# One decode block on one core: wq and w3 each fetched by one DMA instead of two, x by three instead of one

## Chip, core and metric

The kernel runs on one core of a Trainium2 chip. The metric is the device time of one execution in microseconds, the median of the runs shown. Nothing else runs on the core.

## What is computed

One decode step of a transformer block for four sequences, D = 1024, in bf16. The reference, cut to what matters:

```python
# x (4,1,1024); k_cache, v_cache (4,4,8192,128); wq (1024,4096); wo (4096,1024)
# w1, w3 (1024,3584); w2 (3584,1024); Hq = 32, Hkv = 4, Dh = 128
q = layernorm(x) @ wq                        # 32 heads of 128
k, v = the last W = 2048 positions of the caches, each kv head used by 8 q heads
p = softmax(q . k * Dh**-0.5)
h = x + (p . v) @ wo
n = layernorm(h)
out = h + (silu(n @ w1) * (n @ w3)) @ w2
```

Weights and the part of the caches that is read come to 55.6 MB, and every byte of it is used once.

## The kernel before

All big operands go through one SBUF buffer, `ring` (L88), 160 KiB in each of the 128 partitions. `plan` (L110) lists the transfers in their order, each with its place in `ring`; `load_next(n)` (L129) issues the next n entries. Each entry is a DMA from SP's queue through `load_rows` (L90: some consecutive weight rows per partition, in one contiguous run) or two DMAs through `load_kv` (L96: two sequences, 16 KiB per partition each). A place is used again and again, so that an entry may overwrite what an earlier one brought. The framework (Tile) derives waits from the order of the statements in the program and from the bytes of `ring` that they touch: a DMA waits for earlier readers and earlier writers of its bytes, and a matmul waits for the last DMA that stands ahead of it in the program and writes the bytes it reads. DMA completions are counted on eight semaphores, used in rotation over all DMAs of the SP and ACT queues; a DMA whose turn it is waits on SP until the DMA eight before it has landed.

Places in KiB per partition, and the statement at which each entry is issued. The same list for the changed kernel is in the section on the change.

| entry | bytes per partition | issued |
|---|---|---|
| wq rows 0-3, wq rows 4-7 | 0-32, 32-64 | head (`load_next(5)`, L138) |
| k of sequences 0-1, 2-3 | 64-96, 96-128 | head |
| v of sequences 0-1 | 128-160 | head |
| v of sequences 2-3 | 0-32 | in the q loop, after row 3 (L222) |
| wo, 32 rows of 2 KiB | 32-96 | in the k loop, after the 8th unit (L274) |
| w1, 8 rows of 7 KiB | 96-152 | after p.v of sequence 1 (L333) |
| w3 rows 0-3 | 0-28 | after p.v of sequence 3 (L333) |
| w3 rows 4-7 | 28-56 | in the wo loop, after row 11 (L360) |
| w2 rows 0-16 | 56-90 | after the wo loop (L362) |
| w2 rows 17-23, 24-26, 27 | 90-104, 104-110, 110-112 | in the w1 loop, after row 3 (L410) |

Compute runs in this order, each stage on what the previous one left. The layer norm of x (L156 to L174; x is loaded on ACT's queue into `x_sb`, L137, and again as `x_q`, L148). q = xn @ wq, 64 matmuls (L215), in the order of the rows. Sixteen k units: transposes (L263), copies on VectorE and ScalarE (L267, L269), scores (L248). Softmax (L280 to L304). p.v, 64 matmuls for each sequence (L326). The wo product, 128 matmuls in the order of the rows, 4 per row (L353). A second layer norm (L366 to L391). `gate_up` (L398) with w1, 64 matmuls, 8 per row, into `g_ps`; the silu of the gate on ScalarE and VectorE (L415 to L419); `gate_up` with w3 into `u_ps`. Their product and its transpose (L422, L425). The w2 product, 112 matmuls (L433), then the result's cast and store (L443, L444).

Of the kernel before, what the change touches and what calls it, by code (L numbers as in the profile page):

```python
# [19 lines left out]
def kernel(  # L20
# [13 lines left out]
    nc = tc.nc  # L34

    B, _, D = A_x.shape
# [12 lines left out]
    x_flat = A_x.flatten_outer_dims()  # L49
# [31 lines left out]
    RQ = 4  # L81
    BS = 2
    wq_v = A_wq.rearrange("(p i) n -> p (i n)", i=KC)
    wo_v = A_wo.rearrange("(p i) n -> p (i n)", i=IO)
    w1_v = B_w1.rearrange("(p i) n -> p (i n)", i=KC)
    w3_v = B_w3.rearrange("(p i) n -> p (i n)", i=KC)
# [9 lines left out]
    def load_kv(at, src, b):  # L96
# [11 lines left out]
    N_Q, N_F = Hq * Dh, F  # L108
    KIB = 512
    plan = [  # L110
        ("wq", load_rows, (0, wq_v, N_Q, 0, 4)),
        ("wq", load_rows, (32 * KIB, wq_v, N_Q, 4, 4)),
        ("k", load_kv, (64 * KIB, A_k_cache, 0)),
        ("k", load_kv, (96 * KIB, A_k_cache, 2)),
        ("v", load_kv, (128 * KIB, A_v_cache, 0)),
        ("v", load_kv, (0, A_v_cache, 2)),
        ("wo", load_rows, (32 * KIB, wo_v, D, 0, 32)),
        ("w1", load_rows, (96 * KIB, w1_v, N_F, 0, 8)),
        ("w3", load_rows, (0, w3_v, N_F, 0, 4)),
        ("w3", load_rows, (28 * KIB, w3_v, N_F, 4, 4)),  # L120
        ("w2", load_rows, (56 * KIB, w2_v, D, 0, 17)),
        ("w2", load_rows, (90 * KIB, w2_v, D, 17, 7)),
        ("w2", load_rows, (104 * KIB, w2_v, D, 24, 3)),
# [5 lines left out]
    def load_next(n=1):  # L129
        for _ in range(n):  # L130
            if cursor[0] < len(plan):
                kind, f, args = plan[cursor[0]]
                loaded.setdefault(kind, []).extend(f(*args))
                cursor[0] += 1

    x_sb = act.tile([B, D], BF16)
    nc.scalar.dma_start(out=x_sb[:], in_=x_flat)  # L137
    load_next(5)  # L138

    ident = const.tile([P, P], BF16)  # L140
    make_identity(nc, ident[:])
# [5 lines left out]
    for j in range(JG):  # L147
        nc.scalar.dma_start(  # L148
            out=x_q[QD * j : QD * (j + 1) : RS, :], in_=x_flat[:, j * CG : (j + 1) * CG]
# [7 lines left out]
    for c in range(2):  # L157
# [8 lines left out]
        out=xn[:], in0=x_sb[:], scalar1=mv[:, 0:1], scalar2=rstd[:, 0:1],  # L166
# [4 lines left out]
    for kc in range(KC):  # L171
# [15 lines left out]
        out=perm[:].rearrange("p (h dq) -> p h dq", dq=JG),  # L187
        in_=ident[:].rearrange("p (dq h) -> p h dq", dq=JG),
# [12 lines left out]
    for j in range(2, JG):  # L201
        nc.vector.tensor_tensor(
            out=same[:, 0, :], in0=same[:, 0, :], in1=ident[:, j * QD : (j + 1) * QD], op=ALU.add
# [6 lines left out]
    for kc in range(KC):  # L210
        wq_t = loaded["wq"][kc]
        for hf in range(CQ // 512):
            for g in range(JG):
                c0 = g * CQ + hf * 512
                nc.tensor.matmul(  # L215
                    q_ps[QD * g : QD * g + B, hf * 512 : (hf + 1) * 512],
                    lhsT=xnT[:, kc, :],
                    rhs=wq_t[:, c0 : c0 + 512],
                    start=(kc == 0),
                    stop=(kc == KC - 1),  # L220
                )
        if kc == RQ - 1:  # L222
            load_next()
    q_sb = act.tile([P, CQ], BF16)
    nc.vector.tensor_single_scalar(out=q_sb[:, :512], in_=q_ps[:, :512], scalar=qscale, op=ALU.mult)  # L225
    nc.scalar.mul(out=q_sb[:, 512:], in_=q_ps[:, 512:], mul=qscale)
# [1 line left out]
    for r in range(REP):  # L228
        nc.tensor.transpose(out=qt_ps[:, r, :], in_=q_sb[:, r * Dh : (r + 1) * Dh], identity=ident[:])
    nc.vector.tensor_copy(  # L230
        out=qz[:, :, : Hkv * QD].rearrange("p b (g z) -> p b g z", g=Hkv)[:, :, :, :REP],
        in_=qt_ps[:].rearrange("p r (g x) -> p x g r", g=Hkv)[:, :B, :, :],
# [24 lines left out]
    for u, (b, n) in enumerate(units):  # L257
        k_v = loaded["k"][b]
        kT = ktpool.tile([P, NJ, P], BF16, tag="kT")
        for t in range(NJ // TB):  # L260
            kt_ps = psA.tile([P, TB, P], BF16, tag=f"kt{nt % 4}")
            for jj in range(TB):
                nc.tensor.transpose(  # L263
                    out=kt_ps[:, jj, :], in_=k_v[:, n * NJ + t * TB + jj, :], identity=ident[:]
# [21 lines left out]
        out=Pm[:], in_=scores_ps[:], func=ACT.Exp, bias=nmax[:], scale=1.0, accum_out=rsum[:]  # L286
# [6 lines left out]
    for c in range(NSB):  # L293
# [4 lines left out]
        for g in range(Hkv):  # L298
            if g % 2 == 0:
                nc.vector.tensor_scalar(  # L300
                    out=z[:, :, g, :], in0=pt_ps[:], scalar1=mask[:, g : g + 1], scalar2=None, op0=ALU.mult
# [10 lines left out]
        out=Dm[:], in0=ident[:].rearrange("p (g b r) -> p b g r", g=Hkv, b=B),  # L312
# [38 lines left out]
    for i in range(IO):  # L351
# [34 lines left out]
        out=hn[:], in0=h1[:], scalar1=tot[:, 0:1], scalar2=rstd2[:, 0:1],  # L386
# [5 lines left out]
        out=hnT[:].rearrange("p k x -> p (k x)"), in_=hn[:].rearrange("q (c k) -> q k c", k=KC)  # L392
# [5 lines left out]
    def gate_up(kind, out_ps):  # L398
# [27 lines left out]
        out=hgT[:].rearrange("p i x -> p (i x)"),  # L426
        in_=hg[:].rearrange("q s c -> q (s c)").rearrange("q (c i) -> q i c", i=IF),
# [47 lines left out]
```

## Time and profile before

| | us |
|---|---|
| median of 3 runs | 138.12 |
| lowest, highest | 138.05, 138.14 |
| the profiled execution, its own time | 138.12 |
| its span, first to last instruction | 136.3 |
| around the span | 1.8 |
| busy: PE, DVE, ACT, POOL | 67.9, 42.6, 31.0, 1.7 |

All durations below are from the one profiled execution, and times of day in it count from the start of its span. PE is TensorE, DVE VectorE, ACT ScalarE, SP the engine that issues the DMAs of `ring`. In lists of groups and in the timeline a row gives the engine, the line, the operation, its output and inputs, the shapes and how many; in the timeline the first two columns are the start and the length in us, and square brackets hold the idle time of the engine before it and what ended it. In the chain of waits the columns are start, length, and what the time went to. Matmuls overlap, so that the time of a stretch is read from its start and length and not from a mean of one times their number.

### The profile page before, as it was taken

To read this page: it belongs to the slowest core of one execution; us is meant where nothing else is said; L and a number is where in the kernel's file an instruction comes from. 1 tells how busy PE (TensorE), PEld (TensorE's weight loads), DVE (VectorE), ACT (ScalarE), POOL (GpSimd) and SP (SyncE) were. 2 spreads that over 40 slices of the span, in tenths; PEclk is the share of its full clock that TensorE was granted. 3 is DMA by queue.
4 is the path that set the end of the run, shared out by engine and by line. 5 is a ranking of instruction groups with operands and counts; after the bars stand their busy time and mean duration, and the time that the engine had idled before them with its cause. 6 is when DMAs were issued, how large, how long until landed. Compare 5 with 4: busy or idle time off the path is not lost.

```text
span 136.3 us, 2302 instructions
## 1 busy us (share of the span) xinstructions
PE 67.9 (50%) x1035; PEld 42.9 (31%) x1035; DVE 42.6 (31%) x73; ACT 31.0 (23%) x36; POOL 1.7 (1%) x8
## 2 busy tenths in 40 slices
PE   0101803698989889105259538830096440900960
PEld 0100201274656565001149427610043210300840
DVE  6440000244444444609940030160000695070000
ACT  0400000155555646092944000000003300000001
POOL 5000000000000000000000000000000000000000
PEclk9999999999999999965555865897557777555577
DMA  5999899999999999997988989989799999989960
GB/s 156 462 462 443 385 413 418 423 447 423 428 437 409 437 437 423 435 582 341 538 385 365 524 365 442 459 353 522 328 412 463 434 437 447 429 388 409 426 261 5
DMA packets 2662, 55.75 MB, mean 409 GB/s; under 512 B 312, under 2 KB 344, under 8 KB 604
## 3 DMA queue, kind: packets, MB, share of 16 engines
q1 hardware_dynamic: 2592, 55.58, 95.3%
q8 instruction: 8, 0.13, 0.3%
q10 hardware_dynamic: 60, 0.02, 0.1%
q14 instruction: 2, 0.02, 0.0%
HBM read 55.59 MB, written 0.01 MB: 408 GB/s over the span
## 4 chain that ended last, share of the span: by engine, by line
DMA 58%; PE 21%; ACT 13%; DVE 5%; issue 1%; SPq 0%; ACTq 0%
DMA ring<-in_B_w_dram 42%; DMA ring<-in_A_wq_dram 16%; PE kt_ps L263 9%; ACT kT L269 6%; PE scores_ps L248 5%; ACT z L304 3%; PE q_ps L215 2%; PE g_ps L403 2%; DVE rmax L280 2%; ACT Pm L285 2%; PE OT_ps L326 2%; DVE pT L294 1%; DVE z L300 1%; ACT L285 1%; DVE q_sb L225 1%
## 5 line engine op out<-in xcount | busy, mean ns | idle before, releaser
L269 ACT COPY kT<-kt_ps 128x1024 bf16<-128x1024 bf16 x16 | 15.8, 1014 | 12.0 <-PE kt_ps L263 12.0
L263 PE MATMUL kt_ps<-ident,ring 128*128 128x128 bf16 x256 | 16.4, 219 | 0.0
L263 PEld LDWEIGHTS <-ring 128*128 128x128 bf16 x256 | 14.3, 98 | 5.0 <-issue 4.9
L267 DVE COPY kT<-kt_ps 128x1024 bf16<-128x1024 bf16 x16 | 11.1, 691 | 15.2 <-PE kt_ps L263 15.2
L215 PE MATMUL q_ps<-ring,xnT 128*4 128x512 bf16 x64 | 6.7, 596 | 12.0 <-DMA ring<-in_A_wq_dram 12.0
L403 PEld LDWEIGHTS <-hnT 128*32 128x32 bf16 x128 | 5.3, 137 | 23.1 <-issue 20.5
L248 PE MATMUL scores_ps<-kT,qz 128*32 128x512 bf16 x64 | 9.9, 609 | 3.1 <-ACT kT L269 3.1
L326 PE MATMUL OT_ps<-z,ring 128*128 128x32 bf16 x256 | 7.4, 185 | 6.7 <-ACT z L304 5.0
L403 PE MATMUL u_ps<-ring,hnT 128*32 128x448 bf16 x64 | 6.3, 572 | 8.3 <-DMA ring<-in_B_w_dram 8.3
L403 PE MATMUL g_ps<-ring,hnT 128*32 128x448 bf16 x64 | 5.4, 525 | 9.0 <-DMA ring<-in_B_w_dram 9.0
L433 PE MATMUL y_ps<-ring,hgT 128*32 128x256 bf16 x112 | 5.7, 370 | 8.4 <-DMA ring<-in_B_w_dram 8.3
L326 PEld LDWEIGHTS <-ring 128*128 128x128 bf16 x256 | 7.3, 103 | 7.4 <-issue 7.4
L433 PEld LDWEIGHTS <-hgT 128*32 128x32 bf16 x112 | 4.4, 129 | 10.3 <-issue 6.1
L215 PEld LDWEIGHTS <-xnT 128*4 128x4 bf16 x64 | 2.1, 116 | 16.2 <-issue 15.9
L353 PE MATMUL y_ps<-ring,o 128*32 128x256 bf16 x128 | 5.8, 365 | 2.0 <-DMA ring<-in_A_wo_dram 2.0
L443 ACT CAST res<-y_ps 128x256 bf16<-128x256 f32 x1 | 0.4, 372 | 26.5 <-PE y_ps L433 26.5
L304 ACT ACTIVATE z<-pt_ps,mask 128x512 bf16<-128x512 f32 x8 | 5.3, 687 | 3.5 <-DVE z L300 3.5
L225 DVE TENSOR_SCALAR q_sb<-q_ps 128x512 bf16<-128x512 f32 x1 | 0.7, 690 | 17.2 <-PE q_ps L215 17.2
L353 PEld LDWEIGHTS <-o 128*32 128x32 bf16 x128 | 4.8, 130 | 3.8 <-issue 3.1
L300 DVE TENSOR_SCALAR z<-pt_ps,mask 128x512 bf16<-128x512 f32 x8 | 5.5, 740 | 1.2 <-ACT z L304 0.8
L296 PE MATMUL pt_ps<-pT,perm 128*128 128x512 bf16 x4 | 2.4, 607 | 6.8 <-DVE pT L294 6.8
L417 DVE RECIPROCAL eg<-eg 128x896 f32<-128x896 f32 x1 | 5.8, 5753 | 0.0
(73 smaller groups left out, 40.5 us busy)
## 6 DMA issues: line engine op xcount, KB each, us to landing
ring<-in_A_wq_dram SPq DMA_DIRECT2D x2, 4096.0 KB, 16.8
ring<-in_A_k_cache_dram SPq DMA_DIRECT2D x4, 2048.0 KB, 25.5
ring<-in_A_v_cache_dram SPq DMA_DIRECT2D x4, 2048.0 KB, 40.2
ring<-in_B_w_dram SPq DMA_DIRECT2D x1, 7168.0 KB
ring<-in_B_w_dram SPq DMA_DIRECT2D x2, 3584.0 KB, 28.6
ring<-in_B_w_dram SPq DMA_DIRECT2D x1, 4352.0 KB
ring<-in_B_w_dram SPq DMA_DIRECT2D x1, 1792.0 KB
ring<-in_B_w_dram SPq DMA_DIRECT2D x1, 768.0 KB
```

What stands on the lines that cost most here:

```text
L215: nc.tensor.matmul(q_ps[QD * g : QD * g + B, hf * 512 : (hf + 1) * 512], lhsT=xnT[:, kc, :], rhs=wq_t[:, c0 : c0 + 512], start=(kc == 0), ...
L248: nc.tensor.matmul(scores_ps[QD * g : QD * (g + 1), n * 512 : (n + 1) * 512], lhsT=qz[:, b, g * QD : (g + 1) * QD], rhs=kT_v[:, g, :, :], ...
L263: nc.tensor.transpose(out=kt_ps[:, jj, :], in_=k_v[:, n * NJ + t * TB + jj, :], identity=ident[:])
L267: nc.vector.tensor_copy(out=kT[:, t * TB : (t + 1) * TB, :], in_=kt_ps[:])
L269: nc.scalar.copy(out=kT[:, t * TB : (t + 1) * TB, :], in_=kt_ps[:])
L300: nc.vector.tensor_scalar(out=z[:, :, g, :], in0=pt_ps[:], scalar1=mask[:, g : g + 1], scalar2=None, op0=ALU.mult)
L304: nc.scalar.mul(out=z[:, :, g, :], in_=pt_ps[:], mul=mask[:, g : g + 1])
L326: nc.tensor.matmul(OT_ps[:, b, :], lhsT=loaded["v"][b][:, j, :], rhs=PTz[j // NJ][:, (j % NJ) * B + b, :, :], start=(j == 0), stop=(j == J ...
L353: nc.tensor.matmul(y_ps[QD * j : QD * (j + 1), :], lhsT=o4[:, i, :, :].rearrange("p b s -> p (b s)"), rhs=loaded["wo"][i][:, j * CG : (j + ...
L403: nc.tensor.matmul(out_ps[QD * j : QD * (j + 1), hf, :HF], lhsT=hnT[:, k, :], rhs=loaded[kind][k][:, c0 : c0 + HF], start=(k == 0), stop=( ...
L417: nc.vector.reciprocal(out=eg[:], in_=eg[:])
L433: nc.tensor.matmul(y2_ps[QD * j : QD * (j + 1), :], lhsT=hgT[:, i, :], rhs=loaded["w2"][i][:, j * CG : (j + 1) * CG], start=False, stop=(i ...
```

## The change

The two entries of wq become one of 64 KiB per partition, and the two of w3 one of 56 KiB. `x_sb` is filled by three DMAs of 512, 256 and 256 columns. The head issues four entries instead of five, and the call inside the q loop moves behind that loop. The calls at L274, L333, L360, L362 and L410 are as they were.

```diff
-        ("wq", load_rows, (0, wq_v, N_Q, 0, 4)),
-        ("wq", load_rows, (32 * KIB, wq_v, N_Q, 4, 4)),
+        ("wq", load_rows, (0, wq_v, N_Q, 0, 8)),
...
-        ("w3", load_rows, (0, w3_v, N_F, 0, 4)),
-        ("w3", load_rows, (28 * KIB, w3_v, N_F, 4, 4)),
+        ("w3", load_rows, (0, w3_v, N_F, 0, 8)),
...
-    nc.scalar.dma_start(out=x_sb[:], in_=x_flat)
-    load_next(5)
+    for c0, c1 in ((0, 512), (512, 768), (768, D)):
+        nc.scalar.dma_start(out=x_sb[:, c0:c1], in_=x_flat[:, c0:c1])
+    load_next(4)
...
-        if kc == RQ - 1:
-            load_next()
+    load_next()
     q_sb = act.tile([P, CQ], BF16)
```

With 12 entries instead of 14 and the calls that stayed, the entries are issued at these statements:

| entry | bytes per partition | issued, changed kernel |
|---|---|---|
| wq | 0-64 | head (`load_next(4)`) |
| k of sequences 0-1, 2-3, v of 0-1 | as before | head |
| v of sequences 2-3 | 0-32 | after the q loop |
| wo | 32-96 | in the k loop, after the 8th unit |
| w1 | 96-152 | after p.v of sequence 1 |
| w3, 8 rows | 0-56 | after p.v of sequence 3 |
| w2 rows 0-16 | 56-90 | in the wo loop, after row 11 |
| w2 rows 17-23 | 90-104 | after the wo loop |
| w2 rows 24-26, 27 | 104-110, 110-112 | in the w1 loop, after row 3 (the third call finds the list empty) |

## The prediction

> **What bounds the kernel now.** I read the page's slices first, then its chain, then the chain in order of time.
>
> ```profile
> PE   0101803698989889105259538830096440900960
> ...
> PEclk9999999999999999965555865897557777555577
> DMA  5999899999999999997988989989799999989960
> ```
>
> ```profile
> DMA 58%; PE 21%; ACT 13%; DVE 5%; issue 1%; SPq 0%; ACTq 0%
> ```
>
> ```profile
> 1.16 21.35 DMA ring<-in_A_wq_dram
> ...
> 73.22 25.79 DMA ring<-in_B_w_dram
> ...
> 101.59 31.37 DMA ring<-in_B_w_dram
> ...
> 133.35 0.37 ACT res L443
> ```
>
> The DMA row has no hole from the second slice to the last but two, PE's row has many: the kernel lasts as long as 55.6 MB take (408 GB/s over the span), plus a start and a tail. Compute hides as long as each DMA is issued before the stream runs dry. The timeline shows how far each stage is behind its data:
>
> ```profile
> 13.05 3.58 PE L215 MATMUL q_ps<-ring,xnT 128*4 128x512 bf16 x32 [6.05 <-DMA ring<-in_A_wq_dram]
> 22.55 3.15 PE L215 MATMUL q_ps<-ring,xnT 128*4 128x512 bf16 x32 [5.92 <-DMA ring<-in_A_wq_dram]
> 82.25 5.76 PE L353 MATMUL y_ps<-ring,o 128*32 128x256 bf16 x128 [2.04 <-DMA ring<-in_A_wo_dram]
> 91.64 0.63 DVE L391 STREAM_TRANSPOSE hnT<-hn 128x256 bf16<-128x256 bf16 x1
> 115.98 3.17 PE L403 MATMUL u_ps<-ring,hnT 128*32 128x448 bf16 x32 [5.34 <-DMA ring<-in_B_w_dram]
> 126.30 3.82 PE L433 MATMUL y_ps<-ring,hgT 128*32 128x256 bf16 x68 [7.14 <-DMA ring<-in_B_w_dram]
> ```
>
> Every weight stage starts when its DMA lands (brackets). Two arrivals matter below: all of w3 is in by 115.98, w2 rows 0-16 by 126.30. SP's waits show what holds the issues:
>
> ```profile
> SPq L101 <- DMA ring<-in_A_wq_dram: 16.2, 2, 9.9
> SPq L93 <- PE OT_ps L326: 25.3, 2, 20.1
> ```
>
> The first is the rotation of eight completion semaphores (k of sequence 2 waited 9.9 us for wq's first half, though it shares no byte with it). The second is real: w1 and w3 wait for p.v.
>
> **What the Trainium skill says.** "DMA: Bandwidth & Descriptors", Anatomy of one DMA: semaphore waits are made by the issuing sequencer, the DMA engines do not wait. The trace agrees: SP sat 20.1 us on p.v while transfers went on. The same section prices a DMA at about 2.0 us plus its bytes at 436 GB/s. That was fitted on GpSimd's path; here x_sb's 8 KB, issued from ACT at 0.73, released bn_stats at 2.52: 1.79 us, which I use. The same page, Rules for kernel authors, advises at least 1 MiB per DMA for bandwidth. Halves of 4 and 3.5 MB are past that; the trace has 432 GB/s in 22.5 to 25.8 under k's 16 KiB runs and 428 in 82.2 to 88.1 under w1's 56 KiB runs, so longer runs promise nothing.
>
> **The change, part by part.**
>
> *x in three pieces.* Two more issues on ACT at 0.57 us delay the last piece and x_q by 1.2 us. xnT is ready at 7.2, so 8.4; wq now lands at 22.5: hidden by 14 us. Cost 0; without that cover 1.2.
>
> *wq as one DMA.* One DMA has one landing, 22.51, where the second half landed. The 32 matmuls that ran from 13.05 move behind it: q ends at 22.55 + 3.58 + 3.18 = 29.3 instead of 25.74, 3.6 us late, and so do k, softmax and p.v, which are PE and ACT bound. What they hold back is issues: v of 2-3 at about 26 (two rows read) or later, wo 39.7 + 3.6 = 43.3 with v in the stream to 61, w1 73.2 + 3.6 = 76.8 with wo in the stream to 82, w3 79.2 + 3.6 = 82.8 with w1 until 99. Each still meets a stream that is not dry; smallest cover 5 us at w1, less about 1 us from issue to first byte. Cost 0 on the stream.
>
> *The rotation.* With two more x DMAs ahead, the DMA eight places before k of sequence 1 is wq: SP holds it, and k and v behind it, to 22.5. The stream then has only k of sequence 0, 2.1 MB or 4.8 us; the next issue takes 0.6 us and starts about 1 us later. Cost 0. If instead k of sequence 0 falls on wq's semaphore, the stream is dry for about 1.8 us and everything moves by that.
>
> *w3 as one DMA, and the shifted calls.* Here is the cost. The merged entry goes out at L333, ahead of the wo loop in the program, and writes 0-56 KiB; wo's rows 0-11 lie at 32-56. The call after row 11 now issues w2 rows 0-16 into 56-90, wo's rows 12-28; the one after the loop w2 rows 17-23 into 90-104, which takes in w1's row 0 and the start of row 1. The later matmuls therefore read the new bytes (the wo product mostly w3's and w2's numbers, the first two w1 rows partly w2's), and each waits for the DMA that wrote them. That waits follow byte ranges shows in the kernel before: the first 32 q matmuls ran at 13.05 with half of wq outstanding.
>
> 1. w3 behind w1 in the stream: landing 115.98 as before. The wo loop, which began at 82.25, begins there. Queued behind it on PE: everything to the end. Its first 12 rows are 48 matmuls, 48/128 of 5.76 = 2.2 us, to 118.1.
> 2. w2 rows 0-16 need no wo matmul, so SP issues them right behind w3 (about 83): landing 126.30 as before. Rows 12-31, 80/128 of 5.76 = 3.6 us: wo ends at 129.90.
> 3. w2 rows 17-23 must wait for wo's rows 29-31, at 129.90; the stream is dry by then. 1.79 + 1.835 MB at 432 GB/s (4.25) = 6.04: landing 135.95. The second layer norm beside it takes 88.01 to 92.27 = 4.26 us, to 134.2, hidden by 1.8.
> 4. The gate's 64 matmuls, 99.06 to 104.50 = 5.44: 141.4. The last two w2 entries wait for w1's rows 1 and 2 and land before 141; the w2 product is much later.
> 5. The silu, 104.50 to 114.45 = 9.95 (table load, exp, add, a reciprocal of 5.75, product): 151.35. The w3 product, 6.3 us, runs beside it. Before, both hid under the stream.
> 6. L422 and L425, 119.20 to 122.03 = 2.83: 154.2.
> 7. The w2 product without waits, 3.82 + 1.11 + 0.92 = 5.85: 160.1.
> 8. From the last matmul to the span's end, 136.3 − 133.33 = 2.97: 163.05.
>
> The profiled execution takes 1.82 us around its span (138.12 − 136.3) and equals the median, so the sum is **164.9 us**, 26.8 over before.
>
> **Bounds.** Small ones: step 3's fixed part between 1.0 (first issue 0.73, first packets about 1.7) and 2.5 us (the store at 133.75 to the span's end); arrivals ±0.5. PE's pace follows the clock: 56 ns a matmul at clock 0.50 (68 in 3.82), 40 at 0.82 (28 in 1.11); over 80 wo, 64 gate and 112 w2 matmuls −2.5 to +2.0. If w2 rows 0-16 too waited for the wo loop, they would land at 121.7 + 1.8 + 10.3 = 133.8 and rows 17-23 at 138.1: +2.1. The rotation's other place: +1.8. Low 161.0, high 169.0.
>
> **Rivals.**
>
> *The orders do not bind (A).* Should a wo matmul keep its wait for wo's own DMA, or the issues really keep their old order, PE runs as before 3.6 us late. The wo loop begins at 85.9, hnT is at 96 before w1 lands at 99, and the w3 product as one block ends 115.98 + 6.3 = 122.3, its transpose at 125.1, 1.2 us before w2 lands at 126.30: the last landing stays at 132.97 and the time is 138.1, not slower. The point from which it decides: the wo loop must not need anything behind w1 in the stream, that is, start before about 98 (98 + 5.76 + 4.26 + 5.44 + 9.95 + 2.83 = 126.2, when w2 is in). For it: transfers would be the same bytes at the same rate. Against it: the waits seen, byte by byte and by program order. Chance 0.05.
>
> *Only w3's wait binds (B).* If wo waits for w3 but w2's overwriting costs nothing, wo ends at 115.98 + 5.76 = 121.7, w1's product starts at 126.0, ends at 131.4, silu 141.4, then 2.83, 5.85, 2.97: span 153.1, time 154.9. For it: w2 is at place 56 and more, behind w3. Against it: the same rule that binds w3 binds it. Chance 0.05.
>
> *A dry stream at the head (C)*, with all of the forecast: 164.9 + 1.8 = 166.7. It lies in the range. Against it: x's first DMA is issued first, and k of sequence 0 then falls on its semaphore. Chance 0.1.
>
> The forecast itself has 0.8.
>
> **How the numbers follow.** 161 to 169 holds the forecast and C with their bounds; A and B, 0.1, and a miss in size are left out. A measurement of this kernel can tell about 0.2%, 0.3 us; A would be within it mostly, with a little on either side: faster 0.01, same 0.04, slower 0.95.
>
> **What would show it.** Right: L353's first row waits for the DMA of a B weight and starts near 116, a second group near 126; SP waits long on the wo loop; the DMA slices are empty from about 126 to 131 and after 136; the chain ends PE, ACT, DVE (L417) and not in a DMA; L403 starts near 136. At the head, one L215 group of 64 at 22.5. Wrong: L353 starting by 86 (A), L403 by 127 (B), or a hole in the DMA row at 22 to 25 (C).

## Result and profile after

| | before | after |
|---|---|---|
| median, us | 138.13 (138.05 to 138.30, 6 runs) | 165.97 (164.81 to 166.59, 6 runs) |
| the profiled execution, us | 138.12 | 166.07 |
| its span, us | 136.3 | 164.3 |
| HBM read | 55.59 MB | 55.59 MB |

The ratio is 1.2002, 95% interval 1.1955 to 1.2048: the change costs 27.8 us (165.97 − 138.13). Where runs of one kernel lie more than 1.5% apart, its ratio is that of the shorter ones, which below concerns `e4_w3_early_only` alone.

The slices of the page of the changed kernel; each is 4.1 us:

```profile
PE   0000149989898803159300000000602839900192
...
PEclk9999999999999995555955555555595675995559
DMA  7997979999999999999799999998991091510000
```

DMA, which had no hole before, is full up to about 125 us, then comes in pieces, and is idle for the last 16 us. PE is empty from the 21st to the 28th slice, between p.v and wo. The same bytes at the same rate are nearly all in at the same time as before; what follows them is now compute.

The second half of the kernel in the timeline of TensorE:

```profile
116.28 2.75 PE L351 MATMUL y_ps<-ring,o 128*32 128x256 bf16 x48 [33.32 <-DMA ring<-in_B_w_dram]
126.44 4.07 PE L351 MATMUL y_ps<-ring,o 128*32 128x256 bf16 x80 [7.40 <-DMA ring<-in_B_w_dram]
...
134.82 3.92 PE L401 MATMUL u_ps<-ring,hnT 128*32 128x448 bf16 x37 [2.27 <-DVE hnT L389]
138.15 4.40 PE L401 MATMUL g_ps<-ring,hnT 128*32 128x448 bf16 x64
142.20 1.49 PE L401 MATMUL u_ps<-ring,hnT 128*32 128x448 bf16 x27
155.50 5.75 PE L431 MATMUL y_ps<-ring,hgT 128*32 128x256 bf16 x112 [11.81 <-DVE hgT L423]
```

The wo product (L351) began at 82.25 before, released by wo's own DMA. Now PE sits 33.32 us until a DMA of a B weight, w3, lands; then 48 matmuls, which are wo's rows 0-11, and again 7.40 us until w2 rows 0-16 land; then the other 80. By then these DMAs have written over the bytes that the rows 0-28 stood in, so that the product multiplies w3's and w2's numbers: the changed kernel no longer computes the block, and what is timed here is the wait that comes with this. Behind them one stage follows the other without cover, down to the w2 product (L431), which waits 11.81 us for VectorE and for no DMA. Among SP's waits, the issue of w2 rows 17-23 behind the wo loop stands out (us in all, times, longest); before, two waits on the wo product came to 5.5 us:

```profile
SPq L93 <- PE y_ps L351: 31.2, 1, 31.2
```

It ends at 130.55, 4.5 us after the stream ran dry (by the trace's packet records the last packet of w2 rows 0-16 ends at 126.1).

### The profile page after: what moved, and what is told of

Read it like the earlier page. It is cut to its first block, busy times and chain, and to the rows that moved or that the text cites. A ratio compares the mean times of both kernels' runs of the same rounds, so it can differ in the third digit from the quotient of the medians.

```text
span 164.3 us, 2303 instructions
## 1 busy us (share of the span) xinstructions
PE 66.0 (40%) x1035; PEld 41.7 (25%) x1035; DVE 42.5 (26%) x73; ACT 31.1 (19%) x36; POOL 1.7 (1%) x8
## 3 DMA queue, kind: packets, MB, share of 16 engines
HBM read 55.59 MB, written 0.01 MB: 338 GB/s over the span
## 4 chain that ended last, share of the span: by engine, by line
DMA 65%; PE 21%; DVE 8%; ACT 4%; issue 1%; SPq 0%; DVEq 0%; ACTq 0%
DMA ring<-in_B_w_dram 27%; DMA ring<-in_A_wo_dram 25%; DMA ring<-in_A_wq_dram 13%; PE kt_ps L261 4%; PE q_ps L214 4%; PE y_ps L431 4%; DVE eg L415 4%; PE y_ps L351 2%; PE u_ps L401 2%; PE g_ps L401 2%; ACT kT L267 2%; PE scores_ps L246 2%; DVE hgT L423 1%; ACT L413 1%; DVE hg L420 1%
## 5 line engine op out<-in xcount | busy, mean ns | idle before, releaser
L351 PE MATMUL y_ps<-ring,o 128*32 128x256 bf16 x128 | 6.8, 402 | 40.7 <-DMA ring<-in_B_w_dram 40.7
L261 PE MATMUL kt_ps<-ident,ring 128*128 128x128 bf16 x256 | 17.1, 220 | 0.0
L351 PEld LDWEIGHTS <-o 128*32 128x32 bf16 x128 | 5.3, 141 | 43.0 <-issue 42.1
L246 PE MATMUL scores_ps<-kT,qz 128*32 128x512 bf16 x64 | 10.5, 609 | 2.6 <-ACT kT L267 2.6
L431 PE MATMUL y_ps<-ring,hgT 128*32 128x256 bf16 x112 | 5.8, 401 | 11.8 <-DVE hgT L423 11.8
L214 PE MATMUL q_ps<-ring,xnT 128*4 128x512 bf16 x64 | 6.0, 559 | 4.7 <-DMA ring<-in_A_wq_dram 4.7
L431 PEld LDWEIGHTS <-hgT 128*32 128x32 bf16 x112 | 4.3, 143 | 13.5 <-DVE hgT L423 12.2
L171 PE MATMUL tp_ps<-ident,xn 4*128 4x4 bf16 x8 | 0.7, 199 | 17.3 <-DVE xn L164 17.3
L401 PE MATMUL u_ps<-ring,hnT 128*32 128x448 bf16 x64 | 5.4, 483 | 2.3 <-DVE hnT L389 2.3
L401 PEld LDWEIGHTS <-hnT 128*32 128x32 bf16 x128 | 3.9, 121 | 6.9 <-issue 3.0
L171 PEld LDWEIGHTS <-xn 4*128 4x128 bf16 x8 | 0.6, 163 | 17.3 <-DVE xn L164 17.3
```

Source lines behind the costliest of these rows:

```text
L214: nc.tensor.matmul(q_ps[QD * g : QD * g + B, hf * 512 : (hf + 1) * 512], lhsT=xnT[:, kc, :], rhs=wq_t[:, c0 : c0 + 512], start=(kc == 0), ...
L246: nc.tensor.matmul(scores_ps[QD * g : QD * (g + 1), n * 512 : (n + 1) * 512], lhsT=qz[:, b, g * QD : (g + 1) * QD], rhs=kT_v[:, g, :, :], ...
L261: nc.tensor.transpose(out=kt_ps[:, jj, :], in_=k_v[:, n * NJ + t * TB + jj, :], identity=ident[:])
L351: nc.tensor.matmul(y_ps[QD * j : QD * (j + 1), :], lhsT=o4[:, i, :, :].rearrange("p b s -> p (b s)"), rhs=loaded["wo"][i][:, j * CG : (j + ...
L401: nc.tensor.matmul(out_ps[QD * j : QD * (j + 1), hf, :HF], lhsT=hnT[:, k, :], rhs=loaded[kind][k][:, c0 : c0 + HF], start=(k == 0), stop=( ...
L431: nc.tensor.matmul(y2_ps[QD * j : QD * (j + 1), :], lhsT=hgT[:, i, :], rhs=loaded["w2"][i][:, j * CG : (j + 1) * CG], start=False, stop=(i ...
```

## Experiments

Seven kernels. A number of a line is that of the kernel's own text; wo is L351 or L352, the gate and w3 products L399 to L404. The theory is the one of the prediction: the calls that now issue an entry earlier make wo's and w1's products wait for transfers that overwrite their rows. The main rival is that the large DMAs, the late q or the late x cost part of it.

### The calls put back: e1_calls_back

```diff
-        if b % BS == BS - 1:
+        if b == BS - 1:
             load_next()
```

against the changed kernel; wq and w3 stay whole, x stays in three pieces.

> The changed kernel with wq and w3 whole and x in three pieces, but w3 issued in the wo loop after row 11 and w2 rows 17-23 in order behind it: the call at L331 of the changed kernel is made for sequence 1 only. No statement reads overwritten bytes. Theory (the shifted calls cost all of it): wo starts when PE is ready, near 86, the stream has no hole, the last landing stays near 133 and the time is 138.1 to 138.6; w3 as one block leaves some 1 us to w2's landing. Rival (the large DMAs, the late q or the late x cost part of it): q is 3 us later than before, so 141 to 142, or more.

Measured 138.19 us (14 runs, before 138.19 on the same chip), ratio 0.9999, interval 0.9990 to 1.0007. Its timeline of TensorE:

```profile
22.56 5.85 PE L214 MATMUL q_ps<-ring,xnT 128*4 128x512 bf16 x64 [4.59 <-DMA ring<-in_A_wq_dram]
...
83.62 6.06 PE L351 MATMUL y_ps<-ring,o 128*32 128x256 bf16 x128 [0.82 <-DVE o L340]
...
99.05 4.74 PE L401 MATMUL g_ps<-ring,hnT 128*32 128x448 bf16 x64 [7.33 <-DMA ring<-in_B_w_dram]
115.94 4.82 PE L401 MATMUL u_ps<-ring,hnT 128*32 128x448 bf16 x64 [12.16 <-DMA ring<-in_B_w_dram]
126.21 3.62 PE L431 MATMUL y_ps<-ring,hgT 128*32 128x256 bf16 x68 [5.45 <-DMA ring<-in_B_w_dram]
```

All of q waits for the one landing of wq, and q ends at 28.4 instead of 25.7. By wo the delay is 1.4 us (83.62 against 82.25), and at the gate it is gone: 99.05 against 99.06. w3's product, all behind one landing, ends at 120.8, and w2 still arrives at 126.21. The DMAs are those of the change and only the place of a call differs, so the whole loss is in the shifted calls; DMAs of 64 and 56 KiB runs neither gain nor cost more than 0.1% here.

### w3 alone: e2_w3_alone

The kernel before with the two w3 entries merged as in the change, nothing else edited.

> The kernel before with w3 alone merged and nothing else edited, so that all later calls issue one entry earlier, as in the change (the wo product and the first two rows of w1 read overwritten bytes, as there). Theory: the whole loss is here, wo's two groups start at 116 and 126.4, time 165 to 166.5. Rival (wq and x carry part of it): 161 to 163.

Measured 165.65 us, ratio 1.1971 (1.1923 to 1.2019), where the whole change has 1.2002 (1.1955 to 1.2048). wo's groups start at 115.87 and 126.08:

```profile
115.87 2.75 PE L352 MATMUL y_ps<-ring,o 128*32 128x256 bf16 x48 [33.27 <-issue]
126.08 4.46 PE L352 MATMUL y_ps<-ring,o 128*32 128x256 bf16 x80 [7.46 <-DMA ring<-in_B_w_dram]
```

The profile names no releaser for the first wait here; it ends within 0.4 us of where w3's landing ended it in the changed kernel (116.28). The one merged entry, with the calls that it shifts, carries the loss.

### wq and x alone: e3_wq_x_alone

The changed kernel with the two w3 entries of before.

> The changed kernel with w3 in two entries again, so that every later call issues what it did before; wq whole, x in three pieces. Theory: q, k, softmax and p.v run 3 us late, and nothing of it reaches the end: 138.0 to 138.4. Rival (late q pushes w1's issue to where the stream runs dry): 139 to 142, with a hole in the DMA row near 82.

Measured 138.32 us, ratio 1.0007 (0.9998 to 1.0016): no difference. wo starts at 83.72, the gate at 99.23, behind its DMA, and the page's DMA row has no hole near 82, which the rival needed.

### w3 early, w2 late: e4_w3_early_only

```diff
-        if i == 11:
-            load_next()
     load_next()
```

against the changed kernel.

> The changed kernel without the call in the wo loop: w3 still goes out ahead of the wo loop over wo's rows 0-11 (those rows of the product read w3's numbers), but w2 rows 0-16 only after the loop, and the rest of w2 in the w1 loop. Theory: wo starts at 116.2, all 128 matmuls 6.8 us to 123.0; second norm to 127.3, gate to 132.8, silu to 142.7, product and transpose to 145.6; w2 rows 0-16, issued at about 122.4, land by 134.5 to 138 and the rest by 146; end of span 154.5, time 156.3. Rival (w3's overwriting alone makes the loss): 164 to 166.

Measured 154.69 us (median of four runs, 152.86 to 155.81); the ratio, 1.1102 (1.1055 to 1.1148), comes from two of them and is 153.4 us beside 138.19. The timeline is that of the run of 155.19 us:

```profile
116.18 6.27 PE L351 MATMUL y_ps<-ring,o 128*32 128x256 bf16 x128 [33.33 <-DMA ring<-in_B_w_dram]
...
126.77 5.66 PE L399 MATMUL g_ps<-ring,hnT 128*32 128x448 bf16 x64 [2.27 <-DVE hnT L387]
```

wo waits once, for w3, and runs through. The steps behind it come as the sum had them, but the sum, 156.3, is above all four runs. In the profiled one, 1.1 below it, the 128 matmuls took 6.27 us instead of 6.8 and the w2 product 4.92 instead of the prediction's 5.85. So with w3's early issue alone the loss is 15.2 us (153.4 − 138.2), or 16.5 by the median of all four; rival B of the prediction, in which w3's wait alone binds, had 154.9 for the whole time.

### w2 early, w3 in its place: e7_w2_early_only

```diff
-        if b % BS == BS - 1:
+        if b == BS - 1:
             load_next()
...
         if i == 11:
-            load_next()
+            load_next(2)
```

against the changed kernel.

> The changed kernel with w3 issued in the wo loop after row 11, together with w2 rows 0-16, which still come ahead of wo's rows 12-28; w2 rows 17-23 behind the loop as in the change. So w3 overwrites nothing that is read later, w2 rows still do (wo's rows 12-28 and w1's first two read w2's numbers). Theory: wo's rows 0-11 run near 86, rows 12-31 again wait for w2's landing at 126.4, everything behind that as in the changed kernel: 165 to 166.5, no gain from w3's repair alone. Rival (the two waits add): w3's repair gives back the first of them, 138 + about 10 to 17 = 148 to 156.

Measured 165.05 us, ratio 1.1957 (1.1898 to 1.2016), which cannot be told from the change's. Its TensorE:

```profile
83.50 2.75 PE L351 MATMUL y_ps<-ring,o 128*32 128x256 bf16 x48 [0.81 <-DVE o L340]
126.08 4.46 PE L351 MATMUL y_ps<-ring,o 128*32 128x256 bf16 x80 [39.83 <-DMA ring<-in_B_w_dram]
```

The first twelve rows run at 83.50, 33 us earlier than in the changed kernel, and it buys nothing: the 80 that follow wait 39.83 us for w2. The two waits lie one behind the other on the same chain, and the later one contains the earlier. Taking away w3's gains nothing while w2's is there; taking away those of w2 (e4, where rows 17-23 go out late as well) gains 12.6 us (165.97 − 153.4; 11.3 by the median of all four runs); taking away all (e1) gains all.

### No issue behind the wo loop: e6_no_third

```diff
         if i == 11:
             load_next()
-    load_next()
```

against the changed kernel.

> The changed kernel without the call behind the wo loop: w2 rows 17-23 go out in the w1 loop after row 3, with the rest of w2, and no w1 row is overwritten before it is read (wo's rows 0-28 still read w3's and w2's numbers). Theory: wo ends at 130.5 as in the changed kernel, w1's product starts right behind the second norm at 134.8 with no w3 matmuls ahead of it, silu starts at 140.2 instead of 142.6, the w2 product near 153; 163.0 to 164.5, that is 1.5 to 3 below the changed kernel. Rival (the wait on w2 rows 17-23 is what delays the gate by all of the 6 us from 130.5 to landing): more than 3 below. Rival (hidden beside the norm anyway): 165.5 to 166.5.

Measured 163.05 us, ratio 1.1798 (1.1726 to 1.1870). The difference of the ratios, 0.0204, is 2.8 us; the intervals do not meet, so the rival at nothing falls, but they leave 1.2 to 4.4 us, so the time alone does not exclude the rival of more than 3. The timeline does. Its TensorE:

```profile
135.06 6.08 PE L400 MATMUL g_ps<-ring,hnT 128*32 128x448 bf16 x64 [2.27 <-DVE hnT L388]
140.98 3.19 PE L400 MATMUL u_ps<-ring,hnT 128*32 128x448 bf16 x64
```

The gate follows the norm directly, and w3's matmuls all come behind it. It starts 3.1 us before that of the changed kernel (135.06 against 138.15), not 6: the third overwriting adds only what the norm beside it does not cover. In these two executions the gain shrinks to 1.4 us by the gate's end, since the gate took 6.08 us here, at a granted clock of 0.51 (135.0 to 141.1), and 4.40 there, at 0.77 (138.2 to 142.5). The expectation, with a gate of 5.4, had the w2 product near 153; it starts at 154.09.

### x alone: e5_x_alone

The kernel before with x in three pieces, nothing else.

> The kernel before with x in three pieces alone; wq in two DMAs of 32 KiB runs. In the changed kernel x's third piece landed near 14.7 us and its packets came one per 2.43 us on their engines, the length of one 64 KiB packet of wq. Theory (each small packet waits for one packet of the big transfer): here one per 1.2 us, the length of a 32 KiB packet; third piece in by about 9.7, xn ready to be transposed near 12 instead of 17.3, wq's first matmul still near 13; time 138.0 to 138.4. Rival (the pieces themselves are slow, whatever runs beside them): third piece again near 14.7, first q matmul near 18, time still about 138.2.

Measured 138.56 us, ratio 1.0025 (1.0011 to 1.0038). What was to be told apart, when the third piece arrives, is in VectorE's timeline; first the changed kernel, then this one:

```profile
15.22 0.68 DVE L157 BATCH_NORM_STATS2 stats<-x_sb 4x6 f32<-4x512 bf16 x1 [11.67 <-DMA x_sb<-in_A_x_dram]
```

```profile
10.43 0.68 DVE L159 BATCH_NORM_STATS2 stats<-x_sb 4x6 f32<-4x512 bf16 x1 [7.41 <-DMA x_sb<-in_A_x_dram]
```

These are the statistics of the second half of x, which need the second and third piece; before, both halves were under way at 2.52. With 32 KiB runs of wq beside them they start at 10.43, with 64 KiB runs at 15.22. The records of x's packets show why. On one of its engines the second piece's data, its completion, the third's data and its completion start at 7.25, 9.69, 12.11 and 14.55 in the changed kernel, 2.43 apart, and at 6.06, 7.29, 8.51 and 9.74 here, 1.22 apart; a 64 KiB packet of wq takes 2.42 us on its engine, a 32 KiB one 1.21 (medians). From the second piece's data on, each small packet waits for one packet of the big transfer. Why those data start as late as 7.25 and 6.06, which is more than one such packet after their issue, no run shows. The rival, that the pieces are slow in themselves, falls.

The time is 0.1% over what was expected, and the interval excludes 1. The profile gives no place for it: the first q matmul starts at 13.39 instead of 13.05, held 0.27 us by xnT, but the gate is at 99.17 and w2 at 126.34, within 0.15 us of before. The kernels with the same pieces and wq whole show no such excess. It stays open.

## Why the prediction was right

**What bounds it.** That the stream hides compute, and that the position of an issue in the program is what can break it, is what e1 and e3 show. Rival A put the repaired order at 138.1, and e1, which has that order, measured 138.19; its point of decision, wo starting before about 98, is met with 83.62. In the changed kernel itself A does not hold. Rival B, that w2's overwriting costs nothing, fails by e7. Rival C, a dry stream at the head, did not come: k of sequence 1 waited 19.2 us for wq, as the rotation had it, and by the packet records at least 14 of the 16 DMA engines have a packet of the stream in work at any time from 2.2 to 124.1 us. The gate's data were in at 99.05 in e1, which has the same head.

**The sum, step by step** (predicted, measured, us from the start of the span):

| step | predicted | measured |
|---|---|---|
| q done | 29.3 | 28.7 |
| wo, w1, w3 issued | 43.3, 76.8, 82.8 | 41.5, 75.4, 82.4 |
| 1: wo starts, first group's length | 115.98, 2.2 | 116.28, 2.75 |
| 2: second group, wo ends | 126.30, 129.90 | 126.44, 130.51 |
| 3: w2 rows 17-23 transferred in | 4.25 | 5.5 |
| 4: gate, start to end | 135.95 to 141.4 | 138.15 to 142.55 |
| 5: silu's length | 9.95 | 9.95 |
| 6, 7: product and transpose, w2 product | 2.83, 5.85 | 2.83, 5.75 |
| 8: tail | 2.97 | 3.05 |
| span | 163.05 | 164.3 |

The mechanism came as it was forecast: the two groups of wo with their releasers, the issue behind the wo loop, and the bare chain of TensorE, ScalarE and VectorE after it. One sign did not: the DMA row is not empty after 136, because the last two w2 entries, which the prediction had landed before 141, go out at about 141 and end at 144.1. They follow the gate, which came late, and nothing waits for them.

The profiled execution, 166.07 us, is 1.2 above the sum's 164.9, all of it in the span (1.25). That the sum is so near is in part luck, since errors of both signs meet in it. The clock is in the last but two column (the columns are the stretch, its length, busy time and number of instructions of PE, PEld, DVE, ACT and POOL, granted clock, DMA share, GB/s); first the gate before, then the second wo group and the gate of the changed kernel:

```profile
99.10:104.50 5.40, 5.40 (x64) 2.56 (x64) 0.00 (x0) 0.00 (x0) 0.00 (x0) 0.58 1.03 446
```

```profile
126.50:130.50 4.00, 4.00 (x80) 3.16 (x79) 0.00 (x0) 0.00 (x0) 0.00 (x0) 0.57 0.02 4
138.20:142.50 4.30, 4.30 (x76) 2.10 (x72) 0.00 (x0) 0.00 (x0) 0.00 (x0) 0.77 0.29 62
```

- wo ended 0.6 us late. Its second group took 4.07 us instead of 3.6; the granted clock was 0.57, and 0.63 in the row that the prediction took. The first group was 0.55 longer too, but the wait for w2 hides that.
- The gate started 2.2 us late. Of this 0.6 is wo's. The DMA of w2 rows 17-23 adds 0.4: its last packet ends at 137.0, 6.5 us after the issue at 130.55, where the sum had 6.04. The sum's fixed part of 1.79 was too long (the first packet came after 0.95) and its 4.25 for the bytes too short (5.5). The rest, at most 1.1, is 37 matmuls of w3's product ahead of the gate, which the prediction did not have. They need only w3, so the framework's order puts them into the gap; they end at 138.7.
- The gate took 4.40 us instead of 5.44, at a clock of 0.77 instead of 0.58, and gave 1.0 us back. The prediction forecast no faster gate; its bounds for the pace, −2.5 to +2.0, only allowed for one.

Only 27 matmuls of w3's product are left for later, but that end is hidden by the silu in either order.

**x: right in sign, wrong in size.** The step put the delay at two issues, 1.2 us, with xnT at 8.4 and 14 us of cover. xnT is copied from 17.96 to 18.13 in the changed kernel, 10.9 us later than before, and the cover left is 4.6 us. The cost at the end is still nothing, but the term was too small by a factor of nine: it counted the issuing queue and left out the engines' turns. The Trainium skill, "DMA: Bandwidth & Descriptors", section Queues, rings and completion order, says that each DMA engine goes round the queues that have work for it, a packet at a time; the runs agree, with one packet of the stream, 2.43 or 1.22 us, between two small ones.

## What to carry over

Where one buffer is reused and transfers are issued by a counter, merging two entries moves every later issue by one call: write down, for both versions, which entry each call issues and which bytes not yet read it covers, before thinking about bandwidth. A transfer that moves ahead of the reader of the bytes it covers makes that reader wait for the transfer, and for all transfers ahead of it in the queue, and then read the wrong numbers. Several such waits on one chain do not add: removing the earlier one gained nothing while the later one stood (e7), removing the later ones gained 12.6 us (e4). Beside a bulk transfer, each packet of x's second and third DMA waited here for at least one bulk packet, so x came earlier in one DMA than in three (both halves by 2.52, against 10.43 and 15.22), and the longer the bulk runs were, the later it came.

## Not expected of the hardware

A DMA that started in an empty stream was slower than the same bytes inside a busy one. w2 rows 17-23 in the changed kernel:

```profile
131.50:137.00 5.50, 2.86 (x28) 1.22 (x30) 2.18 (x10) 0.29 (x1) 0.00 (x0) 0.67 0.89 331
```

The columns are as above. It moved 331 GB/s where the stream has 432; its packets took 0.63 us each on the mean, the same ones 0.54 in the kernel before. In e6 the same DMA, again first into an empty stream, had 0.63 too; in e4, with w2 rows 0-16 ahead of it, 0.55. The packet records place the loss at the start. The first sixteen packets, one for each engine, took 1.16 us each on the mean in the changed kernel and 1.13 in e6, the 112 that follow 0.55 in both. In e4 it is w2 rows 0-16 that enter an empty stream, and there too their first sixteen packets are long, 1.83 us against 1.30 for the rest. So the bytes are not slower throughout. In the changed kernel the first packet of each engine costs some 0.6 us more, and the engines start up to 0.46 us apart (131.50 to 131.96); together that is most of the 1.25 us by which 5.50 exceeds the 4.25 of a busy stream. Why the first packet is long is not shown.
